# Small attention products on TensorE, issued as two merged steps per unit instead of four

## The chip, the cores and the metric

The kernel runs on one core of a Trainium2 chip. The metric is the device time of one execution in microseconds. Three runs of the kernel before gave 608.38, 611.93 and 609.18 us, median 609.18. A profiled execution is one more run of the same program, recorded by the hardware profiler.

## The reference

Two parts follow each other. The first is a linear attention with a decaying state, for 4 batches, 8 heads, 768 tokens and a head size of 48. The second is a bilinear feed-forward layer on all heads of a token side by side (384 numbers), with 1536 inner columns.

```python
f = 1.0 / (1.0 + np.exp(-f_logit))
for t in range(S):
    state = f[:, :, t, :, None] * state + np.einsum('bhd,bhe->bhde', k[:, :, t], v[:, :, t])
    y[:, :, t] = np.einsum('bhd,bhde->bhe', q[:, :, t], state)
x = y.transpose(0, 2, 1, 3).reshape(B * S, H * D)
out = ((x @ w_a) * (x @ w_b)) @ w_out
```

## The kernel before

**Units and blocks.** The tokens of a batch are cut into two blocks of 384, which makes 8 blocks. A block has two units of four heads each, which makes 16 units, u = 0 to 15. Attention works unit by unit, the feed-forward layer block by block.

**The attention of a unit.** Its front (`front_parts`, L281) turns the gates into running products and scales q by them and k by their inverses: two sigmoids on ScalarE (L294, L291), an affine step on GpSimd (L297), scans on VectorE (L301, L314) and the two products with q and k (L318). Its core has these steps on TensorE:
- `scores` (L356): the products of k and q inside pieces of 64 tokens, 24 small matmuls of 48 rows and 64 columns into the two banks of `ps_x` (L364). VectorE's `mask` (L387) copies them, masked, to `at`.
- `turn` (L391): k is transposed by six 128-wide products into `ps_x` (L399), and ScalarE copies it to `kT` (L409).
- `gains` (L411): k transposed times v, the addition to the state of each piece, 20 or 24 small matmuls into `ps_x` (L423). VectorE's `carry` (L446) adds them up, and `hand_on` (L455) scales the last state for the next block.
- `within` (L457): `at` times v, the product inside a piece, 24 small matmuls into `ps_y` (L466).
- `across` (L475): the states times q, added to the same banks, 20 or 24 small matmuls (L487).

ScalarE copies `ps_y` out (`out_of_bank`, L512), and `stored` (L514) sends y into the block's `xT` by five transfers on SyncE's queue (L531), and then issues the loads of the unit three ahead (L215, L217) on the same queue. There are three sets of q, k, f and v, two buffers of `xT`, and one each of `at`, `kT`, `y` and the output tile `o`.

**The feed-forward layer.** The blocks 0 and 1 use plain products of 128 x 384 (L567). From block 2 on, a fast scheme with fewer products is used. `up_triples` (L683) multiplies sums of weights by sums of x (L689, 120 products of 192 columns per block, each recorded as two matmuls), while ScalarE and VectorE combine what comes out of four banks `ps_f` (L1166, L681). `down` (L764) does the same for the output, 42 products of 192 columns (L782) for a pair of token groups. Its results go to `o` through L797, L804, L807 on ScalarE and L810, L813, L816 on VectorE, and out by two stores on SyncE (L820). `combine_x` (L653) makes the sums of x on VectorE before a block's first product, and GpSimd adds the weight sums once by summing DMAs (L599).

**What sets the order.** The engines work in order, each through its own queue, and the order is made when the program is built. The steps of the feed-forward layer stand in the list `main`. Other work stands in five lines, among them `core` (the steps of `core_parts`, L845) and `fore` (the fronts). Between two steps of `main` the planner's `fill` (L1135) emits the next step of a line. A step on TensorE is emitted where its inputs are ready by the planner's own clock; a step on another engine only if it delays no step of `main` by more than is allowed (`delays`, L1095). Each step carries a load in ns, by which that clock moves on. A step can also have needs (other lines' steps) and a limit `past`, the number of steps of `main` that must stand before it. `scores` of unit s needs the front of s. `across` of a block's first unit waits by `past` until the up-products of two blocks earlier are through, since it leads to a write of their `xT`.

The first four units (`u < 2 * NQ`) run before the planner, in an order written out by hand. The planner's part starts with the core of unit 4 and with the last plain products, near 140 us of the span.

## Time and profile before

| | us |
|---|---|
| median of three runs | 609.18 |
| profiled execution | 608.74 |
| its span, first to last instruction | 606.9 |
| TensorE busy, matmuls | 571.9 |
| TensorE busy, weight loads | 511.7 |
| VectorE busy | 408.3 |
| ScalarE busy | 269.8 |
| GpSimd busy | 75.0 |

The granted clock of TensorE was 0.983 over the span. Up to 140 us the core also loads and converts weights. From there to the end the matmuls run almost without idle time. A matmul's busy time overlaps that of the next, so the rate of a stretch is read from the starts of instructions, not from their lengths. In a row of the timeline the columns are the start in the span, the length, the engine, the line, the operation with its tiles and shape, and the number of instructions merged into the row; a bracket gives the idle time before it and what ended it.

### The profile page before, as it was taken

Reading aid. Unit: us, or ns where it says so; the run is one execution under the profiler, and the core shown is the slowest. Engines: PE = TensorE matmul, PEld = TensorE weight load, DVE = VectorE, ACT = ScalarE, POOL = GpSimd, SP = SyncE. Lnnn points to the kernel's source line nnn. Section 1 sums busy time; section 2 is a strip of 40 time slices with the busy share of each in tenths; the row PEclk is TensorE's granted clock in tenths of the full one; section 3 lists DMA queues with packets and bytes.
Section 4 is the critical chain, followed back from the end, with each engine's and each line's share of the span. In section 5 each row is a group of like instructions: output and inputs, shape, how many; then the busy total and the mean of one; then the engine's idle time right before and its main releaser. Section 6 shows DMA issues by size and latency. Waiting matters only on the chain.

```text
span 606.9 us, 13866 instructions
## 1 busy us (share of the span) xinstructions
PE 571.9 (94%) x5778; PEld 511.7 (84%) x5778; DVE 408.3 (67%) x762; ACT 269.8 (44%) x508; POOL 75.0 (12%) x69
## 2 busy tenths in 40 slices
PE   0769899999989999999999999999999999999995
PEld 0636555556989999999999999999999999999995
DVE  6778444578989689859776866757575265846741
ACT  5567498962332354345433244334431245134300
POOL 5333154534100000000000000000000000000000
PEclk9859999999999999999999999999999999999998
DMA  8887686149744440044004400050001100000000
GB/s 221 236 235 230 154 251 206 46 80 186 137 113 120 126 98 2 2 125 99 1 2 113 124 15 1 2 125 22 1 2 47 46 0 1 1 28 0 1 29 31
DMA packets 33336, 49.42 MB, mean 81 GB/s; under 512 B 3952, under 2 KB 25072, under 8 KB 33264
## 3 DMA queue, kind: packets, MB, share of 16 engines
q1 hardware_dynamic: 29984, 42.38, 25.5%
q0 software_dynamic: 2992, 5.77, 5.6%
q8 instruction: 47, 0.77, 0.6%
q10 hardware_dynamic: 288, 0.30, 0.2%
q14 instruction: 25, 0.20, 0.1%
HBM read 33.23 MB, written 4.72 MB: 63 GB/s over the span
## 4 chain that ended last, share of the span: by engine, by line
PE 91%; DMA 4%; SPq 1%; ACT 1%; DVE 1%; issue 1%; ACTq 0%
PE ps_f L689 39%; PE ps_f L782 27%; PE ps_f L567 15%; PE ps_y L466 2%; PE ps_y L487 2%; PE ps_x L364 2%; PE ps_x L423 2%; DMA f_in<-in_f_logit_dram 1%; PE ps_x L399 1%; DMA xT<-y 1%; DMA k_in<-in_k_dram 1%; DMA out_dram<-o 1%; SPq L215 1%; SPq L211 0%; PE ps_f L487 0%
## 5 line engine op out<-in xcount | busy, mean ns | idle before, releaser
L567 PE MATMUL ps_f<-xT,w_ba 128*128 128x384 f32 x288 | 99.2, 502 | 6.3 <-DVE w_ba L69 4.7
L567 PEld LDWEIGHTS ps_f<-xT,w_ba 128*128 128x128 f32 x288 | 54.9, 195 | 45.8 <-DVE w_ba L69 6.3
L1166 ACT COPY sums<-ps_f 128x384 f32<-128x384 f32 x120 | 57.5, 479 | 71.9 <-PE ps_f L689 66.0
L1166 ACT COPY groups<-ps_f 128x384 f32<-128x384 f32 x120 | 57.7, 481 | 66.9 <-PE ps_f L689 45.0
L689 PE MATMUL ps_f<-xT,w_ba 128*128 128x192 f32 x384 | 78.4, 327 | 0.0
L689 PEld LDWEIGHTS ps_f<-xT,w_ba 128*128 128x128 f32 x384 | 64.9, 190 | 0.2
L689 PE MATMUL ps_f<-groups,w_ba 128*128 128x192 f32 x288 | 55.2, 326 | 0.0
L689 PE MATMUL ps_f<-x_sums,raw 128*128 128x192 f32 x288 | 53.7, 330 | 0.6 <-DVE groups L681 0.4
L782 PE MATMUL ps_f<-w_out,sums 128*128 128x192 f32 x288 | 52.5, 328 | 0.0
L782 PE MATMUL ps_f<-w_out,groups 128*128 128x192 f32 x288 | 51.8, 329 | 0.0
L782 PE MATMUL ps_f<-spare,sums 128*128 128x192 f32 x288 | 50.0, 327 | 0.0
L689 PEld LDWEIGHTS ps_f<-x_sums,raw 128*128 128x128 f32 x288 | 47.1, 190 | 2.8 <-ACT sums L1166 1.7
L689 PEld LDWEIGHTS ps_f<-groups,w_ba 128*128 128x128 f32 x288 | 48.0, 190 | 0.0
L782 PEld LDWEIGHTS ps_f<-w_out,groups 128*128 128x128 f32 x288 | 47.2, 190 | 0.8
L782 PEld LDWEIGHTS ps_f<-w_out,sums 128*128 128x128 f32 x288 | 47.1, 190 | 0.4
L782 PEld LDWEIGHTS ps_f<-spare,sums 128*128 128x128 f32 x288 | 46.9, 190 | 0.3
L59 POOL TENSOR_SCALAR sums<-sums 128x768 f32<-128x768 f32 (+1 forms) x20 | 40.3, 2017 | 50.3 <-ACT sums L57 48.5
L681 DVE TENSOR_TENSOR sums<-sums,groups 128x768 f32<-128x768 f32 x36 | 34.4, 955 | 17.4 <-ACT groups L1166 16.9
L297 POOL TENSOR_SCALAR inv<-inv 128x768 f32<-128x768 f32 x14 | 12.3, 881 | 255.8 <-ACT inv L294 255.8
L681 DVE TENSOR_TENSOR sums<-ps_f,sums 128x384 f32<-128x384 f32 x60 | 32.9, 553 | 15.7 <-PE ps_f L689 14.7
L689 PE MATMUL ps_f<-x_sums,w_ba 128*128 128x192 f32 x192 | 39.9, 330 | 0.0
L689 PE MATMUL ps_f<-xT,raw 128*128 128x192 f32 x192 | 39.5, 328 | 0.0
(123 smaller groups left out, 853.3 us busy)
## 6 DMA issues: line engine op xcount, KB each, us to landing
raw<-w_ba POOLq DMA_DIRECT2D x11, 512.0 KB, 8.3
q_in<-in_q_dram SPq DMA_DIRECT2D x32, 144.0 KB, 4.1
k_in<-in_k_dram SPq DMA_DIRECT2D x32, 144.0 KB, 3.6
v_in<-in_v_dram SPq DMA_DIRECT2D x16, 288.0 KB, 4.7
raw<-in_moe_w_out_dram SPq DMA_DIRECT2D x6, 768.0 KB, 4.2
out_dram<-o SPq DMA_DIRECT2D x24, 192.0 KB, 2.5
f_in<-in_f_logit_dram SPq DMA_DIRECT2D x28, 144.0 KB, 3.1
xT<-y SPq DMA_DIRECT2D x46, 72.0 KB, 2.2
```

The costliest lines, as they stand in the source:

```text
L59: nc.gpsimd.tensor_scalar(h, h, HI_MAX, None, ALU.min)
L215: nc.sync.dma_start(out=t[nm][R * par:R * par + D], in_=heads[par][:, 2 * qd:2 * qd + 2, cols])
L297: nc.gpsimd.tensor_scalar(inv, inv, EXP_K, 1.0, ALU.mult, ALU.add)
L364: nc.tensor.matmul(ps[h][SUB * p:SUB * p + SUB, o:o + SUB], lhsT=kf[r, tokens(n, c, p)], rhs=qf[r, tokens(n, c, p)], start=True, stop=True,)
L423: nc.tensor.matmul(ps_x[R * h:R * h + D, p, (n * NC + c) * D:(n * NC + c) * D + D], lhsT=kT[r, n, c, R * h:R * h + D], rhs=t["v"][r, n, c, ...
L466: nc.tensor.matmul(ps[p][e:e + D, o:o + SUB], lhsT=t["v"][r, n, c, h * D:h * D + D], rhs=at[r, h, o:o + SUB], start=o == 0, stop=True, ski ...
L487: nc.tensor.matmul(ps[p][e:e + D, o:o + SUB], lhsT=st[j][r, n], rhs=qf[r, tokens(n, c, p)], start=False, stop=True, skip_group_check=True,)
L567: nc.tensor.matmul(ps[nm][:, 0:BLK], lhsT=w[:, kt, ft * 128:ft * 128 + 128], rhs=xT[blk][:, kt], start=kt == 0, stop=kt == NKT - 1,)
L681: nc.vector.tensor_tensor(to, x, y, op)
L689: nc.tensor.matmul(ps[:, g], lhsT=sums_of_w[name][:, g, 128 * j:128 * j + 128], rhs=sums_of_x[blk][name], start=start and g == 0, stop=Tru ...
L782: nc.tensor.matmul(to, lhsT=x[:, i // 2, i % 2], rhs=w[:, NI * (i % 2) + i // 2], start=start and i == 0, stop=i == HFT - 1, skip_group_ch ...
L1166: do(*args)
```

## The change

In `core_parts` the step `within` of unit u = s - 1 and the step `scores` of unit s become one step of the planner, `within_and_scores`; `gains` of s and `across` of u become `gains_and_across`. The planner can put nothing between the two halves of a step. Unit 4's `scores` and `gains` stay alone, since unit 3 was finished before, and so do unit 15's `within` and `across`. The need for the front and the limit `past` go to the merged steps, where they now hold back `within` and `gains` too. The loads of the steps, by which the planner's clock moves, are larger than before.

```diff
         u = s - 1
-        if u >= 2 * NQ:
-            yield PE, 850, 20 * BEAT if s == NU else 0, within, u
+        if u < 2 * NQ:
+            yield PE, 1150, 0, scores, s, None
+        elif s < NU:
+            yield PE, 1850, 0, within_and_scores, u
+        else:
+            yield PE, 1050, 20 * BEAT, within, u
         if s < NU:
-            yield PE, 950, 0, scores, s, None
             yield DVE, 880, 0, mask, s
             yield PE, 700, 0, turn, s, None
             yield ACT, 850, 0, turned, s
-        if s < NU:
-            yield PE, 850, 0, gains, s, False
-        if u >= 2 * NQ:
-            yield PE, 800, 0, across, u, False
+        if u < 2 * NQ:
+            yield PE, 1050, 0, gains, s, False
+        elif s < NU:
+            yield PE, 1750, 0, gains_and_across, u
+        else:
+            yield PE, 1050, 0, across, u, False
...
+    def within_and_scores(u):
+        within(u)
+        scores(u + 1, None)
+
+    def gains_and_across(u):
+        gains(u + 1, False)
+        across(u, False)
...
-                    needs=(ready,) if step[3] is scores else (),
-                    past=behind[blk - 2] if step[3] is across and not second else 0,
+                    needs=(ready,) if step[3] in (scores, within_and_scores) else (),
+                    past=behind[blk - 2] if step[3] in (across, gains_and_across) and not second else 0,
```

## The prediction

> **What bounds the kernel now.** I read the share of each engine first, then the chain that ended last, then the order of TensorE in time.

> ```profile
> PE 571.9 (94%) x5778; PEld 511.7 (84%) x5778; DVE 408.3 (67%) x762; ACT 269.8 (44%) x508; POOL 75.0 (12%) x69
> ...
> PE 91%; DMA 4%; SPq 1%; ACT 1%; DVE 1%; issue 1%; ACTq 0%
> ```

> TensorE carries 91% of the chain, so what it costs to *issue* its work counts one for one, and so does each wait in its queue. After 140 us the waits by engine show TensorE waiting 2.2 us in all, and most of that is one wait:

> ```profile
> PE ps_x L423 <- ACT kT L409: 1.5, 1, 1.5
> ```

> The change moves small products among wide ones. TensorE's timeline shows what that interleaving costs. Columns: start, length, line, tiles, shape, count.

> ```profile
> 262.13 2.11 PE L782 MATMUL ps_f<-spare,groups 128*128 128x192 f32 x12
> 264.17 0.89 PE L466 MATMUL ps_y<-at,v_in 64*48 64x64 f32 x48
> 264.88 0.92 PE L364 MATMUL ps_x<-q_in,k_in 48*64 48x64 f32 x48
> 265.73 1.57 PE L782 MATMUL ps_f<-w_out,sums 128*128 128x192 f32 x8
> 267.13 0.82 PE L399 MATMUL ps_x<-ident,k_in 128*128 128x128 f32 x6
> ...
> 336.22 0.81 PE L782 MATMUL ps_f<-w_out,groups 128*128 128x192 f32 x4
> 336.97 0.89 PE L466 MATMUL ps_y<-at,v_in 64*48 64x64 f32 x48
> 337.78 1.57 PE L782 MATMUL ps_f<-w_out,groups 128*128 128x192 f32 x8
> 339.19 4.06 PE L782 MATMUL ps_f<-spare,sums 128*128 128x192 f32 x24
> 343.09 1.46 PE L782 MATMUL ps_f<-spare,groups 128*128 128x192 f32 x8
> 344.48 0.93 PE L364 MATMUL ps_x<-q_in,k_in 48*64 48x64 f32 x48
> 345.34 0.92 PE L782 MATMUL ps_f<-spare,groups 128*128 128x192 f32 x4
> 346.09 0.81 PE L782 MATMUL ps_f<-w_out,sums 128*128 128x192 f32 x4
> ```

> A wide 192-column record starts every 0.1625 us when nothing intervenes (24 records from 339.19 to 343.09); a product is two records, 0.325. I price a stretch of small products as the start of the first wide record that is again in rhythm, less the wide records in between, less the point where the wide work before it would have ended:
> - within alone (L466): from 336.22 + 4 x 0.1625 = 336.87 to 339.19 - 8 x 0.1625 = 337.89, so 1.02.
> - scores alone (L364): from 344.39 to 346.09 - 0.65 = 345.44, so 1.05.
> - the two touching: from 262.13 + 1.95 = 264.08 to 267.13 - 1.30 = 265.83, so 1.75.

> The same reading gives gains alone (L423, at 348.80) 0.88, across alone (L487, at 475.87) 1.02, and the two touching (at 330.21) 1.55. A touching pair therefore saves 0.32 or 0.35 us: one entry (about 0.1) and one return (the first wide record takes 0.43 instead of 0.33, and 0.1 more) instead of two of each. The weight-load side shows the entry as idle time with no releaser:

> ```profile
> 264.17 0.74 PEld L466 LDWEIGHTS ps_y<-at,v_in 64*48 64x48 f32 x48 [0.23 <-issue]
> ```

> [...] the 0.23 us above stands before a 64x48 load that follows wide ones. It stands before no L364 load that follows L466 directly (264.83, no idle). [...] The trace shows weight loads leading by 0.16 us in wide runs and not at an entry. [...]

> **The change, part by part.** Scores of unit s now follow within of s-1 at once, and across of s-1 follows gains of s at once, for s = 5 to 15. It adds and removes no matmul, copy or DMA; it moves them.

> *Fewer stretches.* Counting small products between wide ones in the two orders of TensorE's instructions gives 47 stretches before and 35 after. Of the 11 pairs of each kind, 3 within/scores and 7 gains/across already touched before. New are 8 x 0.32 = 2.56 and 4 x 0.35 = 1.40, together 3.96 us less.

> *The larger loads told to the planner* (850 to 1050, 950 to 1150, pairs 1850 and 1750) cost nothing themselves. They shift where steps fall: the steps of units 4 to 7 move by 2 to 40 wide products, and what VectorE, ScalarE, SyncE and GpSimd issue moves with them. Each needs a look. I number wide products from the first L567; the first L782 is 144.

> *The wait at unit 6's gains.* This is the 1.5 us wait. SyncE's timeline, then ScalarE's:

> ```profile
> 173.07 0.42 SPq L820 DMA_DIRECT2D out_dram<-o  x1
> ```

> ```profile
> 173.27 0.94 ACT L294 ACTIVATE inv<-f_in,less 128x768 f32<-128x768 f32 x1 [3.52 <-DMA f_in<-in_f_logit_dram]
> ...
> 174.33 0.84 ACT L291 ACTIVATE f_in<-f_in 128x768 f32<-128x768 f32 x1
> 176.77 0.32 ACT L804 COPY o<-ps_f 128x192 f32<-128x192 f32 x1 [1.59 <-DMA out_dram<-o]
> 176.98 0.81 ACT L409 COPY kT<-ps_x 128x768 f32<-128x768 f32 x1
> ```

> There is one buffer o. Its last row was stored at 173.07, behind y's and the next unit's transfers on SyncE's queue, and landed at about 176.7. L804 waits for that, L409 stands behind L804, and gains (177.84) wait for L409. In the changed order ScalarE has L804, L294, L807, L291, L409: both sigmoids now stand *behind* the wait. The first store of that queue follows VectorE's L816. In the new order a scan (0.87) and L681 stand ahead of it, so L816 ends near 165.15 against 164.88, and what hangs on it shifts 0.27: L804 at 177.04. Then L294 0.84, its read of the sum 0.22, L807 0.21 and L291 0.75 (spacings of starts at 154.35 to 156.16) put L409 at 179.27 and gains at 180.13, by the 0.86 from L409 to gains before. TensorE gets there itself at 177.54: product 144 starts at 149.36 - 1.02 = 148.34, since within of unit 4 has left its place at 147.79; then 70 wide products (22.75), three pairs (1.75 + 1.55 + 1.75), two turns of 0.65 and an entry of 0.1. The wait is 2.59 instead of 1.53, so 1.06 more. Bounds: if the store landed 2.6 earlier it would be nothing (1.5 gained), and with landing times as scattered as 1.8 to 3.9 for SyncE's transfers to xT, 1 us more is possible.

> *Queued behind it.* VectorE's scans of unit 7 wait for L291 to near 179.4, and L810 behind them, which frees the bank for product 216. L810 ends near 180.6, TensorE needs it at 182.2: hidden. The y copies then run 2.7 later than before, so xT's transfers go 183.05 to 186.1 and land by 188.2. The combination of x that needs them ends near 196.5, and block 2's first up comes near 203.7: hidden by 7 us. The two stores of the second pair, also behind SyncE's loads, land 2.7 later, near 195.4. L804 waits for them, then L813, and behind L813 on VectorE stands L318 for unit 7's k. Its end, near 197.4, meets scores of unit 7 at 197.3: 0.1 us, with no cover left.

> *GpSimd* issues one summing DMA after L297 instead of before it (137.2 becomes about 141.4). The sums in it are read at 171 or later, and the last of these DMAs, issued at 154.11, has 15 us to land (longest 13.1). Nothing.

> *Gains of units 9, 11, 13, 15* now wait with across until xT may be overwritten (the limit `past`). Carries follow across in both orders, so no reader comes later; y copies and x sums have over 50 wide products (16 us) of cover. Nothing. *within* now also waits for the next unit's front, and its own reader across comes later still. Nothing.

> Sum: -3.96 + 1.06 + 0.1 = -2.8 us. The profiled execution took 608.74 for a span of 606.9; span 604.1, execution 605.9. The median before is 609.18, 0.44 above the profiled one, so 606.4 by the same difference.

> **Rivals.**
> *A, the whole gain.* The store lands early enough or other small waits go as well: VectorE's before 292.45 (0.38) and ScalarE's before 250.62 (0.25) stand where core work has moved away. -4.0 or more: 605.2 down to 604.5. For it: TensorE's other waits are tiny. Against: L409 behind L804 and both sigmoids is fixed by the order.
> *C, the wait grows.* Landings 1 to 3 us later meet unit 6's gains and unit 7's scores twice: -2 to +0.5, so 607.2 to 609.7. For it: no cover at either place. Against: the queue pattern ahead of the store is unchanged.
> *D, slower.* VectorE's mask (L387) waits for scores, which within now delays by 0.71 (264.17 to 264.88), with all VectorE work behind it. If TensorE paid this at all 11 units it would cost 7.8 against 3.96: +3.9, 613.1. It loses from 0.36 per unit on. For it: VectorE is in order and waited 6.8 us for scores between 140 and 300 us. Against: a wait of 3.15 us at 265.83 cost TensorE nothing, and the wide work that needs VectorE next is itself held up by the same 0.71.
> *E, no gain from touching*: excluded by the pairs that touch already.

> **How the numbers follow.** Main case 0.45 (saving 2 to 3.6), A 0.27, C 0.17, D 0.11. A measurement of this kernel tells about 0.5%, here 3.05 us, from no change. A and a third of the main case lie beyond it: faster 0.42. Two thirds of the main case and C: same 0.47. D: slower 0.11. The range 603.8 to 610.5 leaves out D and the far end of A.

> **What would show it.** Stretches: 12 fewer idle entries of 0.23 on the weight-load side, and L466 followed by L364 without wide records from unit 5 on. The wait of L423 for L409 near 2.6 us, with L294 and L291 between L804 and L409. Scores of unit 7 waiting 0 to 0.5. Block 2's first L689 near 203.7 instead of 204.72. Waits of TensorE for VectorE in the up stage beyond 1 us together would speak for D. The prediction is wrong if the wait at L423 differs by over 1 us or a pair saves under 0.2.

## The result, and the profile after

Twelve runs each on one chip gave 612.79 us for the kernel after (610.59 to 614.22) and 610.39 for the kernel before (608.38 to 611.93): ratio 1.0043, 95% interval 1.0029 to 1.0058. A later set of runs gave 1.0043 again (1.0026 to 1.0060). The change costs 2.6 us, where 2.8 us of gain were forecast. The profiled execution has a span of 610.6 us, 3.7 more than before.

The page of the kernel after, its busy times and its chain of what ended last:

```profile
PE 572.2 (94%) x5778; PEld 512.7 (84%) x5778; DVE 409.4 (67%) x762; ACT 269.9 (44%) x508; POOL 75.1 (12%) x69
...
PE 85%; DMA 6%; DVE 3%; ACT 2%; issue 2%; SPq 1%; ACTq 0%; DVEq 0%
```

The busy times are those of before within 1.1 us, but TensorE's share of the chain fell from 91% to 85%. So TensorE waits more. Its waits after 143 us (line waited at, what for, us in total, times, longest):

```profile
PE ps_x L423 <- ACT kT L409: 2.2, 1, 2.2
PE ps_x L399 <- DVE at L387: 0.9, 1, 0.9
PE ps_f L689 <- ACT groups L1180: 0.8, 1, 0.8
PE ps_f L689 <- DVE sums L681: 0.4, 2, 0.2
PE ps_f L689 <- ACT sums L1180: 0.2, 1, 0.2
```

4.5 us against 2.2. (Lines past 844 are 14 higher here: L1180 is L1166 of before.) That is not all of it, since each restart behind a wait costs about 0.1 us more that carries no releaser (the four wide records from 218.30 take 0.76 us from start to start, 218.30 to 219.06, instead of 0.65). So I read the starts of the wide products at the stage boundaries from TensorE's timeline. The table runs from the first wide product behind unit 4's scores (140.25 in the profile of before, 142.19 after) to the last matmul row. A ends at block 2's first L689, B is block 2's up stage, C runs to block 4's first L689, D is the rest.

| us | A | B | C | D | sum |
|---|---|---|---|---|---|
| before | 64.47 | 47.56 | 97.20 | 248.95 | 458.18 |
| after | 64.92 | 50.02 | 96.31 | 248.70 | 459.95 |
| after, second profile | 65.05 | 50.21 | 96.31 | 248.71 | 460.28 |

The sum is 1.8 and 2.1 us longer. The other 1.9 us of the two first profiles lies ahead of the table, where TensorE's instructions are the same: that start fell anywhere between 140.25 and 142.94 in the profiles of this study, the two ends both without any join (before and run 9), so it is no effect of the change.

**The saving is there.** TensorE's matmuls and weight loads of a joined step in block 2 (`within` of unit 7, `scores` of unit 8):

```profile
213.71 0.89 PE L466 MATMUL ps_y<-at,v_in 64*48 64x64 f32 x48
214.41 0.92 PE L364 MATMUL ps_x<-q_in,k_in 48*64 48x64 f32 x48
215.26 0.92 PE L689 MATMUL ps_f<-xT,w_ba 128*128 128x192 f32 x4
```

```profile
213.70 0.74 PEld L466 LDWEIGHTS ps_y<-at,v_in 64*48 64x48 f32 x48 [0.23 <-issue]
214.36 0.83 PEld L364 LDWEIGHTS ps_x<-q_in,k_in 48*64 48x64 f32 x48
```

The rhythm is that of the touching pair of before (0.70 and 0.85 between starts, 0.71 and 0.85 before), and only the first of the two has the 0.23 us of entry.

**The wait at unit 6's gains** has the form that was forecast. ScalarE's timeline: the copy to `o` waits, and both sigmoids and the copy to `kT` stand behind it.

```profile
178.90 0.32 ACT L804 COPY o<-ps_f 128x192 f32<-128x192 f32 x1 [8.43 <-DMA out_dram<-o]
179.11 0.94 ACT L294 ACTIVATE inv<-f_in,less 128x768 f32<-128x768 f32 x1
...
180.04 0.31 ACT L807 COPY o<-ps_f 128x192 f32<-128x192 f32 x1
180.24 0.85 ACT L291 ACTIVATE f_in<-f_in 128x768 f32<-128x768 f32 x1
180.99 0.80 ACT L409 COPY kT<-ps_x 128x768 f32<-128x768 f32 x1
```

**Behind it TensorE ran at half clock,** which was not forecast. First its timeline, then the granted clock in slices of 1 us (behind the slice and its length stand the busy times of PE, PEld, DVE, ACT and POOL with their counts, then PEclk):

```profile
181.84 0.70 PE L423 MATMUL ps_x<-v_in,kT 64*48 64x48 f32 x38 [2.16 <-ACT kT L409]
...
183.18 1.64 PE L782 MATMUL ps_f<-spare,sums 128*128 128x192 f32 x4
184.62 3.11 PE L782 MATMUL ps_f<-spare,groups 128*128 128x192 f32 x12
```

```profile
183.00:184.00 1.00, 1.00 (x16) 0.92 (x7) 0.90 (x4) 0.66 (x2) 0.00 (x0) 0.61 0.08 16
184.00:185.00 1.00, 1.00 (x5) 1.00 (x4) 0.24 (x2) 0.77 (x2) 0.00 (x0) 0.50 0.00 0
185.00:186.00 1.00, 1.00 (x5) 1.00 (x4) 1.00 (x2) 0.00 (x0) 0.00 (x0) 0.50 0.25 71
186.00:187.00 1.00, 1.00 (x6) 1.00 (x5) 0.95 (x2) 0.00 (x0) 0.00 (x0) 0.69 0.29 72
```

Four wide records took 1.64 us, where at the same place run 2 below has 0.92. From 187 on the clock is 1.00 again.

**In block 2's up stage** I counted the excess of each group of wide products over its rhythm (0.1625 us per record and 0.1 at each restart): 2.9 us of waits, against 0.4 before. One is 1.0 us (216.66 to 218.30, for ScalarE), the others are some ten of 0.05 to 0.4. Block 3 has 1.6 instead of 0.65, most of it the wait for the mask.

The ledger of the first profile closes, with the forecast price for the pairs: 3.96 saved, 0.63 lost at the gains, about 1.6 by the half clock, 2.5 in block 2, 0.95 in block 3. That gives +1.7, where the table has +1.8.

### The profile page after: what moved, and what is told of

Its sections match the earlier page's. It is cut to its first block, busy times and chain, and to the rows that moved or that the text cites. A ratio compares the mean times of both kernels' runs of the same rounds, so it can differ in the third digit from the quotient of the medians.

```text
span 610.6 us, 13870 instructions
## 1 busy us (share of the span) xinstructions
PE 572.2 (94%) x5778; PEld 512.7 (84%) x5778; DVE 409.4 (67%) x762; ACT 269.9 (44%) x508; POOL 75.1 (12%) x69
## 4 chain that ended last, share of the span: by engine, by line
PE 85%; DMA 6%; DVE 3%; ACT 2%; issue 2%; SPq 1%; ACTq 0%; DVEq 0%
PE ps_f L689 36%; PE ps_f L782 26%; PE ps_f L567 15%; DMA xT<-y 2%; PE ps_y L487 2%; PE ps_y L466 1%; PE ps_x L423 1%; PE ps_x L364 1%; DMA f_in<-in_f_logit_dram 1%; PE ps_x L399 1%; DMA k_in<-in_k_dram 1%; DVE sums L681 1%; DMA out_dram<-o 1%; SPq L215 1%; DMA q_in<-in_q_dram 1%
## 5 line engine op out<-in xcount | busy, mean ns | idle before, releaser
L567 PE MATMUL ps_f<-xT,w_ba 128*128 128x384 f32 x288 | 100.1, 506 | 6.9 <-DMA xT<-y 3.7
L567 PEld LDWEIGHTS ps_f<-xT,w_ba 128*128 128x128 f32 x288 | 55.1, 195 | 47.2 <-issue 7.4
L1180 ACT COPY groups<-ps_f 128x384 f32<-128x384 f32 x120 | 57.7, 481 | 66.6 <-PE ps_f L689 43.0
L1180 ACT COPY sums<-ps_f 128x384 f32<-128x384 f32 x120 | 57.6, 480 | 64.0 <-PE ps_f L689 56.6
L689 PE MATMUL ps_f<-xT,w_ba 128*128 128x192 f32 x384 | 78.6, 327 | 0.8 <-ACT groups L1180 0.8
L689 PEld LDWEIGHTS ps_f<-xT,w_ba 128*128 128x128 f32 x384 | 64.7, 190 | 1.5 <-ACT groups L1180 1.1
L689 PE MATMUL ps_f<-groups,w_ba 128*128 128x192 f32 x288 | 55.2, 327 | 0.0
L689 PE MATMUL ps_f<-x_sums,raw 128*128 128x192 f32 x288 | 53.8, 330 | 0.4 <-ACT sums L1180 0.2
L782 PE MATMUL ps_f<-spare,sums 128*128 128x192 f32 x288 | 51.7, 332 | 0.0
L782 PE MATMUL ps_f<-w_out,sums 128*128 128x192 f32 x288 | 51.6, 327 | 0.0
L782 PE MATMUL ps_f<-w_out,groups 128*128 128x192 f32 x288 | 51.2, 328 | 0.0
L689 PEld LDWEIGHTS ps_f<-x_sums,raw 128*128 128x128 f32 x288 | 47.1, 190 | 2.8 <-ACT sums L1180 1.7
L689 PEld LDWEIGHTS ps_f<-groups,w_ba 128*128 128x128 f32 x288 | 48.0, 190 | 0.4 <-ACT groups L1180 0.2
L782 PEld LDWEIGHTS ps_f<-spare,sums 128*128 128x128 f32 x288 | 47.4, 192 | 0.5
L782 PEld LDWEIGHTS ps_f<-w_out,groups 128*128 128x128 f32 x288 | 47.2, 190 | 0.6
L782 PEld LDWEIGHTS ps_f<-w_out,sums 128*128 128x128 f32 x288 | 47.2, 190 | 0.3
L681 DVE TENSOR_TENSOR sums<-sums,groups 128x768 f32<-128x768 f32 x36 | 34.4, 955 | 14.8 <-ACT groups L1180 14.4
L297 POOL TENSOR_SCALAR inv<-inv 128x768 f32<-128x768 f32 x14 | 12.3, 881 | 258.4 <-ACT inv L294 258.3
L681 DVE TENSOR_TENSOR sums<-ps_f,sums 128x384 f32<-128x384 f32 x60 | 32.9, 554 | 13.9 <-PE ps_f L689 12.5
L689 PE MATMUL ps_f<-x_sums,w_ba 128*128 128x192 f32 x192 | 39.3, 327 | 0.2 <-DVE sums L681 0.2
L689 PE MATMUL ps_f<-xT,raw 128*128 128x192 f32 x192 | 39.3, 327 | 0.0
```

Of the source, the lines that this page charges most:

```text
L297: nc.gpsimd.tensor_scalar(inv, inv, EXP_K, 1.0, ALU.mult, ALU.add)
L567: nc.tensor.matmul(ps[nm][:, 0:BLK], lhsT=w[:, kt, ft * 128:ft * 128 + 128], rhs=xT[blk][:, kt], start=kt == 0, stop=kt == NKT - 1,)
L681: nc.vector.tensor_tensor(to, x, y, op)
L689: nc.tensor.matmul(ps[:, g], lhsT=sums_of_w[name][:, g, 128 * j:128 * j + 128], rhs=sums_of_x[blk][name], start=start and g == 0, stop=Tru ...
L782: nc.tensor.matmul(to, lhsT=x[:, i // 2, i % 2], rhs=w[:, NI * (i % 2) + i // 2], start=start and i == 0, stop=i == HFT - 1, skip_group_ch ...
L1180: do(*args)
```

## The experiments

All were timed against the kernel before on the same chip, in four sets (runs 1 to 4, 5 to 8, 9 to 11, and 12); the kernel before had medians of 610.11, 609.40, 609.58 and 609.55 us in them. "Sum" is the last column of the table above, from one profile each. The theory to begin with (Q) was that the joins push waiting work ahead of other work in the queues of ScalarE and SyncE. The rival (D, from the prediction) was that a joined step makes VectorE's mask late. A third (P, position) came up after the first four runs.

**1. Only gains and across joined.**

```diff
-            yield PE, 1850, 0, within_and_scores, u
+            yield PE, 900, 0, within, u
+            yield PE, 950, 0, scores, s, None
```

> Only gains and across become one step; within and scores stay two steps as before. The built order has 32 stretches of small products in the planner's part instead of 36 before and 24 after, and ScalarE's and SyncE's orders around unit 6 and 7 are those of before (both sigmoids ahead of the copy to o, y's transfers of unit 6 ahead of the third pair's stores). Theory Q (the queues: joining within to scores pushes waiting work ahead of other work on ScalarE and SyncE, and that costs more than the pairs save): 4 pairs x 0.35 = 1.4 us faster than before, ratio 0.9977, TensorE's wait at unit 6's gains 1.5 as before, clock 1.00 there, waits in the up stage of blocks 2 and 3 near 0.9 together. Theory D (joined small products hold back VectorE): these pairs hold back across and y, not the mask, so also -1.4. Theory N (a touching pair saves nothing in net): 0, ratio 1.000.

Measured: 610.26 against 610.11, ratio 1.0003 (0.9991 to 1.0015), sum 457.95. A miss of 1.4 us. Stage B was 48.88, 1.3 more than before, though ScalarE's and SyncE's orders around units 6 and 7 were the old ones. Up to unit 9's `scores` the steps stand within 4 products of their old places, while the `gains` of unit 9 move from product 332 to 390, behind `past`. This run does not separate the two. But one of its waits, ahead of the L689 row at 228.78, comes before the old place of these gains, so small shifts alone can make block 2 wait.

**2. The first pair's stores on GpSimd's queue.**

```diff
-            nc.sync.dma_start(out=out[...], in_=got["o"][:, i])
+            queue = nc.gpsimd if pair == ((0, 1), (0, 2)) else nc.sync
+            queue.dma_start(out=out[...], in_=got["o"][:, i])
```

> The kernel after, with the two stores of the first pair of token groups issued from GpSimd's queue instead of SyncE's, so that the second is not behind y's transfers and the loads. Theory Q with the clock: the store lands some 6 us earlier, the wait of 2.2 us at unit 6's gains falls below 0.6, the granted clock stays 1.00 at 180 to 187 us, and with it go the 1.7 us of products at half clock: -3 to -3.9 against after, ratio to before 0.998 to 0.9965... from 612.8 to about 609.2. Rival: the half clock has another cause than the idle time; then it stays (or comes elsewhere) and only the wait goes, -1.6 to -2.2, 610.9. Theory D: the wait was small beside the mask's delay; less than 1 us, 612. The waits in the up stage of blocks 2 and 3 stay near 3.4 in Q and D.

Measured: 608.23, ratio 0.9977 (0.9961 to 0.9994), sum 456.01, A 61.19 instead of 64.92. GpSimd's timeline shows the second store at 169.23, where SyncE had issued it at 174.34. TensorE's timeline at unit 6's gains has neither wait nor half clock:

```profile
179.67 0.70 PE L423 MATMUL ps_x<-v_in,kT 64*48 64x48 f32 x38
...
181.01 0.92 PE L782 MATMUL ps_f<-spare,sums 128*128 128x192 f32 x4
181.77 2.11 PE L782 MATMUL ps_f<-spare,groups 128*128 128x192 f32 x12
```

So the store behind y's transfers on SyncE's queue costs 3.7 us of A, the wait and what follows it. B stayed at 49.79.

**3. The third pair's stores on GpSimd's queue** (the same edit for the pair `((1, 1), (1, 2))`).

> The kernel after, with the two stores of the third pair issued from GpSimd's queue, so that y's transfers of unit 6 and the loads of unit 9 on SyncE no longer stand behind them. Theory Q: the transfers go near 201 instead of 209, the sigmoid of unit 9 no longer waits for its load to 217, TensorE's wait for ScalarE near 217 (0.8) and the one for the mask near 293 (0.9) go, and all waits in the up stage of blocks 2 and 3 fall from 3.4 to about 0.9: -2.5, 610.3, ratio 1.000. Theory D (the mask comes late because scores come after within): the waits stay above 2.5, less than 0.8 us is gained, 612 or more. The wait at unit 6's gains and the half clock stay in both.

Measured: 611.56, ratio 1.0028 (1.0013 to 1.0044), sum 460.37, B 50.22. Theory Q fails for the up stage. SyncE's queue in the kernel after, and then in this run:

```profile
190.95 17.67 SPq L820 DMA_DIRECT2D out_dram<-o  x4
208.97 3.41 SPq L531 DMA_DIRECT2D xT<-y  x5
```

```profile
189.98 0.89 SPq L821 DMA_DIRECT2D out_dram<-o  x2
207.14 3.41 SPq L531 DMA_DIRECT2D xT<-y  x5
```

With no store of the third pair ahead of them, y's transfers still start 1.86 us after block 2's first L689 (205.28 here), just as after (208.97 - 207.11). The stores stood in the queue but held nothing up: y itself is late, because unit 6's across stands later.

**4. Both pairs' stores on GpSimd's queue.**

> The kernel after with both store pairs on GpSimd's queue. Theory Q: both gains add, -5.5 to -6.4 against after, 606.4 to 607.3, ratio to before 0.9935 to 0.995: the 4 us of the joined pairs come out at last. Theory D: -4 at most, 608.8. If GpSimd's own work is held up by its waits for the stores (the affine step of a front behind them), less than 4 is gained and new waits for inv show on VectorE.

Measured: 608.66, ratio 0.9990 (0.9969 to 1.0012), sum 455.90. No more than run 2 gave, as run 3 would have it. GpSimd's affine steps were not held up to any effect.

**What the order of the built programs says.** Counting wide products from the first L567, the steps stand as follows.

| first product behind the step | before | after |
|---|---|---|
| within 4 / scores 5 | 143 / 162 | 164 |
| within 5 / scores 6 | 184 / 194 | 206 |
| within 6 / scores 7 | 220 / 230 | 260 |
| within 7 / scores 8 | 266 / 272 | 290 |
| within 8 / scores 9 | 296 / 324 | 354 |
| gains 9 | 332 | 390 |
| within 10 / scores 11 | 446 / 464 | 478 |

(In the column "after" both halves have one place.) `scores` touched `within` before only where the next front was ready. A joined step always waits for that front, and not only `within` comes later: `scores` does too, by 2 to 30 products, and with it mask, gains, y, the loads three units ahead and the next fronts. The larger loads told to the planner are not what moves them: in run 10 below, which keeps the old loads, the joined steps of units 4 to 8 stand at the same 164, 206, 260, 290 and 354. Theory P: these now meet the feed-forward layer's own copies and sums where ScalarE and VectorE have no slack.

**5. The halves of the joined step swapped.**

```diff
-        within(u)
         scores(u + 1, None)
+        within(u)
```

> The kernel after with the two halves of the joined step swapped: scores of the next unit first, within behind it. The scheduler's order of everything else is the same, and VectorE's mask gets its scores 0.7 us earlier. Theory D (the joined step makes the mask late, and VectorE's queue behind it): the waits of TensorE in the up stage of blocks 2 and 3, 3.4 us in all, fall to about 1: 2.4 us faster than after, ratio to before 1.0003. Theory P (position: the joined step waits for the front of the next unit, so that it, y, the loads and the next fronts move to places where ScalarE and VectorE have no slack): the mask near 293 stands behind a sum on VectorE and not behind the scores, so nothing or at most 0.3 us: ratio 1.0035 to 1.0043, the waits stay.

Measured: 611.51, ratio 1.0063 (1.0038 to 1.0088), sum 459.34. The time lies above both forecasts, though its interval reaches that of P; the sum is 0.6 below that of after and does not show why. The swap brings the scores forward, but not the mask. There is one `at`: the mask of unit s writes it, so it must also wait until `within` of s - 1 has read it. VectorE's mask of unit 8, in the kernel after and then in this run:

```profile
215.37 0.96 DVE L387 TENSOR_TENSOR at<-ps_x,causal 128x768 f32<-128x768 f32 x1 [1.21 <-PE ps_x L364]
```

```profile
214.21 0.96 DVE L387 TENSOR_TENSOR at<-ps_x,causal 128x768 f32<-128x768 f32 x1 [1.23 <-PE ps_y L466]
```

The joined step starts at 213.71 and 212.55, so the mask comes 1.66 us behind it in both; only what it waits for has changed, from `scores` (L364) to `within` (L466). So this run does not test theory D, and it cannot refute it. Two things in the traces speak against D where its loss was read. The wait for the mask near 293 did not come from the scores: in the kernel after that mask (292.89) starts without idle time, right behind a sum on VectorE. And the largest wait in block 2 is still the one for ScalarE (0.6 us here, 0.8 in the kernel after), which run 6 takes up.

**6. f's load ahead of y's transfers.**

```diff
+        if u >= 2 * NQ:
+            load_unit(u + NSET, "f")
...
-            load_unit(u + NSET)
+            load_unit(u + NSET, "kqv" if u >= 2 * NQ else "fkqv")
```

> The kernel after, with the load of f for the unit three ahead issued ahead of y's five transfers on SyncE instead of behind them. Theory P: the sigmoid of unit 9 on ScalarE, which waited 3.8 us for this load with the copies out of ps_f behind it, finds it 3.4 to 3.9 us earlier, so TensorE's wait of 0.8 to 1.0 near 217 goes: block 2's up stage from 50.0 to about 49.0, -1.0 in all, 611.8, ratio 1.0025; the wait for the mask near 293 stays. If that sigmoid is held up by something else, or if y's transfers, now 1 us later, are late for the sums of x, nothing is gained or a wait at a block's first product shows.

Measured: 610.53, ratio 1.0025 (1.0008 to 1.0042), B 48.65 instead of 50.02, sum 456.43. Unit 9's sigmoid on ScalarE, in run 4 and then in this run:

```profile
213.15 0.94 ACT L294 ACTIVATE inv<-f_in,less 128x768 f32<-128x768 f32 x1 [3.76 <-DMA f_in<-in_f_logit_dram]
214.09 0.46 ACT L1181 COPY groups<-ps_f 128x384 f32<-128x384 f32 x1
```

```profile
210.12 0.94 ACT L294 ACTIVATE inv<-f_in,less 128x768 f32<-128x768 f32 x1
211.06 0.47 ACT L1182 COPY groups<-ps_f 128x384 f32<-128x384 f32 x1
```

The mask of unit 8 stands as it stood, behind the joined step, so D does not explain this gain. This is one path of P from end to end: across of unit 6 comes late, so y and the load behind it do, the sigmoid waits 3.8 us for the load, and the copies out of `ps_f` queue behind the sigmoid. The largest wait of block 2 is gone; a rest of 1.5 us and the wait for the mask remain. (A was 62.76: in this profile the wait at the gains was 1.67 and the clock stayed at 1.00.)

**7. The joins for units 10 to 14 alone.**

```diff
+        ws, ga = s < NU and u in (10, 11, 12, 13, 14), s < NU and u in (10, 11, 12, 13, 14)
+        if ws:
+            yield PE, 1800, 0, within_and_scores, u
...
+        if ga:
+            yield PE, 1650, 0, gains_and_across, u
```

> The kernel before with both joins only for within and across of units 10 to 14, with the old loads added. All steps up to unit 10 stand where they stood before; 3 new pairs of within and scores and 3 of gains and across, 3 x 0.32 + 3 x 0.35 = 2.0 us less. Theory P: the loss came with units 4 to 9, here nothing waits more: -2.0, 608.3, ratio 0.9967; if the wait for the mask at unit 11 (0.9) comes here too, -1.1, 0.9982. Theory D: the mask is late in each of the 3, 3 x 0.7 = 2.1 lost, ratio 1.000. The wait at unit 6's gains is 1.5 to 2.0 as before, the clock there 1.00.

Measured: 608.07 against 609.40, ratio 0.9980 (0.9967 to 0.9993), sum 455.86, 2.3 less than before. B is 47.56, the old value, and TensorE's waits after 143 us are as few as before:

```profile
PE ps_x L423 <- ACT kT L409: 1.2, 1, 1.2
PE ps_f L689 <- ACT sums L1182: 0.3, 1, 0.3
```

By its time (-1.2 us by the ratio) it falls 0.8 short of the -2.0 expected. No wait for the mask came, though unit 11's scores stand at product 476 here and at 478 after: the fronts around it are in their old places. This is also the test of D that run 5 was not: in three more pairs the mask now stands behind `within` and `scores` (unit 11's at 286.70, 1.52 us of VectorE's idle time before it), and TensorE waits no more than before. For the late units D is refuted; for the early ones it is not tested.

**8. The same with the first pair's stores on GpSimd's queue.**

> The joins for units 10 to 14 alone, as in the run before, and the two stores of the first pair of token groups on GpSimd's queue. The wait at unit 6's gains (1.5 to 2.0 in the kernel before) goes with the earlier store: -2.0 and -1.5 to -2.0 together, -3.5 to -4, 606.2 to 606.9, ratio 0.9935 to 0.9943. In theory D -1.5 to -2 alone, ratio 0.997.

Measured: 606.52 against 609.40, ratio 0.9954 (0.9941 to 0.9967), sum 454.27, 3.9 less than before. The profile shows no wait of TensorE for another engine after 143 us. By its sum it meets the expectation, by its time (-2.9) it falls 0.6 short of it. It is the fastest kernel of the study and beats both.

**9. Control: the kernel before with that store alone.**

> Control: the kernel before, with nothing joined, and the two stores of the first pair of token groups on GpSimd's queue. If the wait at unit 6's gains hangs on that store in the kernel before as well, its 1.2 to 1.5 us go and nothing else changes: -1.2 to -1.5, ratio 0.9975 to 0.998, planner's part of the profile 456.7 to 457.0 against 458.2. Then the joins themselves, with the same store (0.9977 in the earlier run), were worth only 0 to -0.7 us: their 4 us are eaten in the up stages. If instead the gain of that earlier run came from the joins, this control stays at 1.000.

Measured: 608.01 against 609.58, ratio 0.9972 (0.9958 to 0.9985), sum 456.29. The earlier stores are worth 1.7 us to the kernel before. Run 2, with the joins and the same stores, had 0.9977, well within the two intervals: so without the wait at the gains, all joins together are worth nothing that can be told. Against run 8 (454.27), the late joins alone are worth 2.0 us by the sums, the 3 x 0.32 + 3 x 0.35 of the price, and 1.1 us by the ratios (0.9954 against 0.9972).

**10. The joins for units 4 to 9 alone** (the edit of run 7 with those numbers).

> The complement of the late joins: both joins only for within and across of units 4 to 9, old loads added. 5 new pairs of within and scores and 1 of gains and across, 5 x 0.32 + 0.35 = 1.95 us less. Theory P: all of the loss is here: the wait at unit 6's gains near 2.2 (+0.6), half clock behind it if the idle time is above 2.05 (+1.6), block 2's up stage near 49.8 instead of 47.56 (+2.2): +2.5, 612.5, ratio 1.003 to 1.0045. The wait for the mask at unit 11 may not come, since unit 11's steps stand elsewhere. If the loss comes from the joins in general, it is half of the change's: +1, and late joins would have lost as well, which they did not.

Measured: 613.77 against 609.58, ratio 1.0073 (1.0054 to 1.0092), sum 460.65, 2.5 more than before. This is more than was expected (1.003 to 1.0045). The early joins lose at least what the whole change does; B is 49.83. The wait at the gains was 3.1 us, and behind it the clock did *not* drop:

```profile
182.29 0.70 PE L423 MATMUL ps_x<-v_in,kT 64*48 64x48 f32 x38 [3.08 <-ACT kT L409]
...
183.64 0.92 PE L782 MATMUL ps_f<-spare,sums 128*128 128x192 f32 x4
184.39 2.11 PE L782 MATMUL ps_f<-spare,groups 128*128 128x192 f32 x12
```

The time is 4 us above before, the sum 2.5. The profiled execution was the fastest of the six (612.03, mean clock 0.984). Four of the other five had a mean clock of 0.979 to 0.981, where none of the 28 executions of before in this set was below 0.982; 3.4 us more at half clock lower it by 0.0028. That hints at the half clock in these four. It is not shown, since none of them was profiled, and a longer half clock at the start lowers the mean too (the one in the first 48 us is 17.07 us long in this run's profile and 20.48 in that of the kernel after).

**11. The kernel after with both cures** (runs 2 and 6 together).

> The kernel after with both cures: the first pair's stores on GpSimd's queue, and f's load ahead of y's transfers. If they add: planner's part -2.2 (the store alone) and -1.4 (block 2's up stage in the run with f first) against before, -3.6; time -3 to -3.6, 606.4 to 607, ratio 0.994 to 0.995, the wait for the mask near 290 (0.9) still there. If they overlap: -2.2, ratio 0.9965.

Measured: 607.94 against 609.58, ratio 0.9969 (0.9957 to 0.9981), sum 455.31, B 48.65. The cures mostly add in the profile (2.9 of 3.6) and less so in time: 0.9969 against 0.9977 with the store alone. It is no better than the control with the stores alone (0.9972), and by the sums 1.0 better (455.31 against 456.29), where the pairs were priced at 3.96: the two cures leave most of the loss in the up stages in place.

**12. The kernel after, once more.**

> The kernel after, unchanged, once more. The half clock behind the wait at unit 6's gains came in the runs with 2.16, 2.36 and 2.09 us of it and not with 2.04, 1.67 or 3.08. If it follows from the length of the wait, a wait above 2.1 gives it again and one of 3 us would have; if it hangs on where the wait falls in a time base of its own, it may be missing at the same 2.2 us, and the stage from the first L782 to block 2's first L689 then takes 55.2 instead of 56.8. The up stages of blocks 2 and 3 stay at 50.0 and 46.4, the time at 612 to 613, ratio 1.003 to 1.006.

Measured: 612.35 against 609.55, ratio 1.0043 (1.0026 to 1.0060), sum 460.28. The wait was 2.13 us and the half clock came again (four wide records behind it took 1.65 us). B was 50.21.

## Why the prediction was wrong

- **Base.** 606.4 rested on 609.18, the median of three runs. The later sets gave 609.4 to 610.4 for the kernel before. About 1 us of the 6.4 us error is this.
- **Fewer stretches, -3.96: right in the profiles.** The pairs have the forecast rhythm, runs 8 and 9 put six of them at 2.0 us by the sums (1.1 by the times), and the ledger closes with this price for all twelve.
- **The wait at unit 6's gains: right in its mechanism, its size a little off.** 2.16 and 2.13 us instead of 2.59. This profile started 1.94 us late (142.19 against 140.25). Less that, L409 started at 179.05, where 179.27 was forecast, mostly because the sigmoids followed L804 more closely; and TensorE came to the gains at 177.74 instead of 177.54. Each makes about half of the difference.
- **"Queued behind it ... block 2's first up comes near 203.7": wrong.** Less the late start it came at 205.17, 1.5 late. L810, y and the combination of x were indeed hidden; what I had not counted was that the products behind the wait run at half clock. In four profiles with it (after twice, runs 3 and 5), A is longer than in run 6, which had none, by 1.5 to 1.8 us beyond the longer wait. The prediction took a wait for its own length.
- **Unit 7's scores, 0.1; GpSimd, nothing: right.** No wait shows at either.
- **The step that failed most, a term put at nothing: "*within* now also waits for the next unit's front, and its own reader across comes later still. Nothing", and "Gains of units 9, 11, 13, 15 ... Nothing".** I asked who reads `within` and `across`, and found cover. I did not ask where `scores` goes, which moves with it, nor what moves with `scores`. The prediction said that the steps of units 4 to 7 move, and what the other engines issue with them, and followed this only as far as unit 7's scores. Units 8, 9 and 11 move too, and the y, loads, sigmoids and sums of these units meet block 2's and block 3's up stages, where 3.4 us were lost instead of nothing. Runs 7 and 10 show that the loss comes with the early joined steps: with these in their old places six pairs gain 2.3 us by the sum, with the early ones joined 2.5 us are lost. How it comes about is shown for one path (run 6, 1.4 us); for the rest it is argued from the order.
- **Rival D gave 613.1, close to the time, by luck as far as the runs show.** It charged all 11 units, and run 7 has late units where the mask is held back just so and TensorE loses nothing; the half clock (1.6) and the load of run 6 (1.4), which D does not have, are 3.0 of the ledger's 5.7 us of losses. I wrote that waits for VectorE in the up stage "would speak for D". They came (0.9 us for the mask), but the mask there stood behind a sum on VectorE, that behind ScalarE's copies, and those behind a sigmoid that waited for `inv` (L294 at 290.23, 1.06 us for L318). The sign was not sharp enough to name D. This last chain I only read in the trace; no run took it away by itself.
- **The chances.** C ("the wait grows") and D together had 0.28, and only D's lay clearly above the time before. The case that came, stalls in the up stage from shifted positions, had none.

Not settled: how much of the 2.6 us falls to the half clock in executions that were not profiled; which of block 2's ten small waits hangs on which moved step, since only the largest was taken apart; and whether the mask, held back as D has it, has a part in these small waits of the early units (at most the 1.1 us that run 6 leaves in B).

## What to carry to other kernels

A fused step inherits the latest of its inputs, so price not only the fused instructions but the whole chain behind the half that is held back, its loads and the next unit's preparation, over every stage in which they now land. Where a scheduler fills the gaps of a full engine, change what is cheap to place (here the late units, where the joins earned their price by the profiles and about half of it by the times) and leave the tight stage as it is. And a store that shares a queue with transfers can hold a single output buffer long enough to stall the bound engine: moving one pair's two stores was worth 1.7 us to the kernel before.

## What the hardware showed that I had not expected

In these profiles the changes of the clock lie whole multiples of 3.41 us apart. In the kernel after it rose near 46.7 us, fell at 183.2 and rose again at 186.6: the drop is 3.41 us long, and the fall comes 136.5 us, 40 times 3.41, behind the rise. Run 3 and the second profile of after have the same 136.5. The stretch at 0.50 that ends near that first rise is 20.48 us long in the kernel after (6 times 3.41) and 17.07 in the kernel before (5 times). If each profile is cut into windows of 3.41 us, laid out from its own changes of the clock, the longest part of the wait that falls into one window puts the nine in order:

| profile | wait | most of it in one window | clock in the next window |
|---|---|---|---|
| run 3 | 2.36 | 2.36 | 0.50 |
| after, second profile | 2.13 | 2.13 | 0.50 |
| run 5 | 2.09 | 2.09 | 0.50 |
| after | 2.16 | 2.04 | 0.50 |
| run 10 | 3.08 | 1.90 | 1.00 |
| run 6 | 1.67 | 1.67 | 1.00 |
| run 1 | 2.04 | 1.37 | 1.00 |
| run 7 | 1.24 | 1.24 | 1.00 |
| before | 1.53 | 0.82 | 1.00 |

The 3.08 us of run 10 fell across an edge between two windows, 1.90 and 1.18. Over all profiles of this study, from 60 us to near the last products, only these four windows have more than 1.90 us without a matmul, and only behind these four does the clock fall. In the first 60 us the order does not hold: in the kernel before the clock falls behind a window with 1.86 us idle. So idle time alone is not the whole condition. The windows were laid over the traces afterwards, and no run placed a wait on purpose: why the clock falls is not shown.
